# Windowed attention and a two-layer MoE product on one core: the globals of the second pair by one-hot products, three V casts moved ahead, and a split last store

## The chip, the cores and the metric

One core of a Trainium2 chip. The metric is the device time of one execution in microseconds (us), median of several runs. The engines are TensorE (PE, matrix products into PSUM), VectorE (DVE), ScalarE (ACT), GpSimd (POOL) and SyncE (SP, which here only issues transfers). Each works through its own instructions in order and waits on semaphores for the others. Transfers are issued from the queues of SP, ACT and GpSimd.

## The reference

```python
# q, k, v: (8, 8, 576, 64) float32; global_idx: 8 positions
scores = (1 / sqrt(64)) * q @ k.T                    # per batch and head
mask   = (|i - j| <= 32) | is_global[i] | is_global[j]
attn   = softmax(where(mask, scores, -1e9))
x      = (attn @ v) as (4608, 512)                   # heads side by side
r      = max(x @ w_in, 0)                            # w_in: (512, 2048)
out    = (s * r * r + b) @ w_out                     # w_out: (2048, 512)
```

## The kernel before

**Attention.** Two heads make a pair; a batch has 4 pairs, and there are 32 pairs in 8 batches. A pair's 576 positions go in 5 chunks of 120 keys, and each chunk's 128 partitions are 8 global keys and 120 own keys. `qk(p, s)` is the score product of chunk s (K columns as weights, Q of both heads as the moving operand), followed by `exp` on ACT into `e`; the product with the 0/1 mask on DVE into `em` is put off to the next step. `pv(p, parts)` sums over the chunks: part 0 with V (`vring`) as weights, the value product, and part 1 with ones, the sums, both into the one PSUM tile `po`. `norm_steps` turns the sums to reciprocals by two ACT steps (`ln`, `rep`), and DVE writes the normalised columns into `xt`. The 8 global queries of a batch are handled apart and put into `xt` by GpSimd in `scatter`, 8 small copies, once the batch's fourth pair is normalised.

**K and Q** of pairs 0 to 7 are loaded in bf16 as `six` and turned by PE: `trans_a` (K) and `trans_b` (Q), each 12 transposes into PSUM `pst`, then copies into `kt` (DVE, L444) and `qbd` (L460, one half by ACT and one by DVE). Q is kept block-diagonally in three buffers `qbufs`. Pairs 8 and on come by another way (`natk`, `natq`, rounded on ACT at L182).

**The globals' columns** of K and Q have to stand in every pair's `kt` and `qbd`. For pair 0 they are made by `select_first`: products of `six` with a one-hot matrix `sel6` (L678), copied from PSUM by DVE (L684, L689). For all later pairs `gather` fetches the global rows of all heads in a half of the batches by indirect DMA (`gf`), DVE rounds them (`gb`, L368, L387), PE turns them (L375), ACT copies them out as `gkt` and `gqd` (L379, L382), and `put_kq(p)` copies a pair's share into place (DVE, L415, L419). The global rows of V go through 16 small PE products (L394) into `gvx` (ACT, L396).

**V** of a pair is loaded as float32 into `natv` (ring of 4), cast into `vring` (ring of 4) by `cast_v` on ACT or GpSimd (L216), and then `put_v` writes the 8 global rows over it: by DVE, or (engine `None`) by a small SP transfer (L408).

**Order.** All is written out by hand; no scheduler moves anything. A list `later` holds what is to be issued one step later, and `now` what is issued at the end of the same step. Pair 0 to 4 run their five score steps in `first_pair`, without MoE work between; from there `run_pair` runs 8 steps (5 with scores, 3 with turning and casts), and `Q(n)` sets pieces of MoE work between them. `first_pair` also issues `warm`, products of a dummy tile of 512 columns whose results nobody reads. In order, the stretch in question is: turning of pair 0, one-hot products, masks; `first_pair(0)` with the rounding and turning of the gathered globals; the V globals; then GpSimd's transfers, and for pairs 1 to 3 a GpSimd cast followed by an SP transfer of the global V rows. GpSimd's queue between them holds the transfers of `win_t` (`moe_w_in`, two of 1 MB), `natv`, `six`, `wout_t`, and eight reads of the global positions into registers (L810). Software transfers of GpSimd wait for the one eight places before them.

**MoE.** Tokens go in tiles of 512: 16 products `psh` (L566) with ReLU on ACT (L573) and squaring on DVE (L576), then 4 output rows of 128 tokens `pso` (L581), each 16 products of 512 columns, scaled and biased on DVE into `osb` (L601) and stored by SP (L605).

Of the kernel before, what the change touches and what calls it, by code (L numbers as in the profile page):

```python
# [12 lines left out]
OP = mybir.AluOpType  # L13
# [53 lines left out]
def kernel(  # L67
# [385 lines left out]
    def trans_b(p, later=later):  # L453
        ps = trans("q", p)

        def evac():
            n = HB // NJ
            for hh, eng in ((1, nc.scalar.copy), (0, nc.vector.tensor_copy)):
                r = slice(D * hh, D * hh + D)
                eng(  # L460
                    out=view(qbufs[p % 3][r, hh], [P, NCH], [HB + NG, 2], [NJ, n], [1, NJ]),
                    in_=view(ps[r], [2 * n, NCH], [n, 2], [1, n], [NP6, NJ]),
                )

        later.append(evac)
# [85 lines left out]
    def moe_quanta():  # L551
        for t in range(NTOK // 512):
            c0 = 512 * t
            gl = []
            cols = []
            a = c0
            while a < c0 + 512:
                x0 = a % (NX * S)
                n = min(c0 + 512 - a, NX * S - x0)
                cols.append((x0, a - c0, n))  # L560
                a += n
            for f in range(16):
# [12 lines left out]
                gl.append(g)  # L575
                later.append(lambda g=g, r=r: nc.vector.tensor_mul(g[:], r[:], r[:]))  # L576
                yield
            for u in range(4):
                pso = ps_m.tile([P, DM], FP32, tag="moe", name="pso")
                for f in range(16):  # L580
                    nc.tensor.matmul(  # L581
                        pso[:], gl[f][:, u * P : u * P + P], wout_t[:, f],
                        start=(f == 0), stop=(f == 15),
                    )
                    if f % 4 == 3 and f < 15:
                        yield

                def store(pso=pso, r0=c0 + u * P, t=t):
                    if t < 3:
                        i = r0 // P  # L590
                        if i < 8:
                            osb = held.tile([P, DM], FP32, tag=f"held{i}", name="osbh")
                        else:

                            osb = six["kq"[i // 11]].rearrange("p n h j d -> p (n h j d)")
                            osb = osb.bitcast(FP32)[:, DM * ((i - 8) % 3) :][:, 0:DM]
                        held_rows.append((osb, r0))
                        nc.vector.tensor_scalar_mul(out=osb[:], in0=pso[:], scalar1=s_bc[:])
                        return
                    osb = mop.tile([P, DM], FP32, tag="osb", name="osb")  # L600
                    nc.vector.scalar_tensor_tensor(  # L601
                        out=osb[:], in0=pso[:], scalar=s_bc[:], in1=bias_row[:],
                        op0=OP.mult, op1=OP.add,
                    )
                    nc.sync.dma_start(out=out[r0 : r0 + P, :], in_=osb[:])  # L605

                later.append(store)
                yield

# [21 lines left out]
    def run_pair(p, nq, extra, turn):  # L631

        bi, hp = divmod(p, 4)
        if hp == 0 and p > 4:
            open_batch(bi)
        for s in range(8) if p > 4 else range(NCH, 8):
            prev, later[:] = list(later), []
            now = []
            if s < NCH:
                qk(p, s)  # L640
                if s in (1, 2):
                    step()
                if s == 4 and hp == 0 and bi > 1:
                    later.append(lambda: scatter(bi - 1))
                if s == 2 and p + 1 < NSIX:
                    cast_v(A, p + 1)
                if s == 2 and NSIX <= p + 2 < NPAIR:
                    cast_v(G, p + 2)
            elif s == 5:
                if p == 4:  # L650
                    cast_v(A, 5)
                if 4 < p < NSIX - 1:
                    trans_b(p + 1, now)
                elif turn:
                    turn_q(turn, now)
            elif s == 6 and 4 < p < NSIX - 1:
                trans_a(p + 1, now)
            for f in now + prev:
                f()
            if s == 0:  # L660
                pv(p - 1)
                pending.extend(norm_steps(p - 1))
            if s == 6 and p + 1 < NSIX:
                put_v(V, p + 1)
            for f in extra.get(s, ()):
                f()
            Q(nq[s])
# [1 line left out]
    def idle_bank():  # L669
        return ps_m.tile([P, DM], FP32, tag="moe", name="psw")  # L670

    def select_first():

        ps = ps_m.tile([P, 2, NG], FP32, tag="moe", name="psg")
        for i, t in enumerate("kq"):
            for j in range(NJ):
                for hh in range(2):
                    nc.tensor.matmul(  # L678
                        ps[D * hh : D * hh + D, i], six[t][:NP6, 0, hh, j], sel6[:NP6, j],
                        start=(j == 0), stop=(j == NJ - 1), skip_group_check=True,  # L680
                    )

        def put():
            nc.vector.tensor_copy(  # L684
                out=view(ktile[0], [P, NCH], [1, NG]), in_=view(ps[:, 0], [0, NCH], [1, NG])
            )
            for hh in range(2):
                r = slice(D * hh, D * hh + D)
                nc.vector.tensor_copy(  # L689
                    out=view(qbufs[0][r, hh, HB:], [P, NCH], [1, NG]),  # L690
                    in_=view(ps[r, 1], [0, NCH], [1, NG]),
                )

        later.append(put)
# [7 lines left out]
    def first_pair(p, extra={}):  # L702


        if p % 4 == 0:
            open_batch(p // 4)
        bank = idle_bank()
        for s in range(NCH):
            prev, later[:] = list(later), []
            now = []  # L710
            if p or s > 1:
                warm(1, bank)
            qk(p, s)
            if p == 4 and s > 2 or p < 4 and s < 2:
                (trans_b, trans_a)[1 - s % 2 if p == 4 else s](p + 1, now)
            if p and s in (1, 2 if p == 4 else 3):

                pv(p - 1, (int(s == 1),))
                if s == 1:
                    pending.extend(norm_steps(p - 1))  # L720
            if s == 3 and p < 4:
                step()
            for f in prev + now:
                f()
            for f in extra.get(s, ()):
                f()
            if s == 1:
                step()
                if p == 4:
                    step()  # L730
            if s == 4 and p == 4:
                put_v(V, 4)

    warm(8)
    trans_a(0)
# [22 lines left out]
            load_kq(4)  # L758
    clear(qbufs[1][0:D, 1], LQ)
    clear(qbufs[1][D:P, 0], LQ)  # L760
    select_first()
    flush()
    warm(3)
    vkey = const.tile([P, NCH], FP32)
# [21 lines left out]
    def clear_q2():  # L786
# [1 line left out]
        nc.vector.memset(qbufs[2][D:P, 0], 0.0)  # L788

    first_pair(0, {  # L790
        1: [lambda: cast_v(A, 0), lambda: build_masks((2,)), steps0[0]],
        2: [lambda: build_masks((3, 4))],
        3: [steps0[1], steps0[2]],
        4: [clear_q2, lambda: put_kq(1)],
    })
    for f in steps0[3:]:
        f()
    flush()
    put_v(V, 0)
    load_v(nc.gpsimd, 4)  # L800
    load_kq(5)
    cast_v(G, 1)
    put_v(None, 1)
    for p in (1, 2, 3, 4):
        first_pair(p)
        if p == 1:
            load_v(nc.gpsimd, 5)
            load_w_out(0)
            greg_p = [
                nc.gpsimd.value_load(g32[:1, i, 0:1], min_val=0, max_val=S - 1)  # L810
                for i in range(NG)
            ]
            cast_v(G, 2)
            put_v(None, 2)
        elif p == 2:
            load_kq(6)
            load_v(nc.gpsimd, 6)
            cast_v(G, 3)
            put_v(None, 3)
        elif p == 3:  # L820
            load_w_out(1)
            cast_v(G, 4)
    flush()
    scatter(0)
    for i in (1, 2, 3):
# [136 lines left out]
```

## Time and profile before

| | us |
|---|---|
| Median of 11 runs | 372.35 (371.67 to 373.1) |
| The profiled execution | 370.75 |
| its span | 369.1 |
| PE busy | 340.7 (92%) |
| DVE, ACT, POOL busy | 237.5, 227.3, 84.3 |

The span runs from the first instruction to the last event of the profile. Times in the views are counted from its start. A slice is a fortieth of the span, and a digit is the busy share in tenths. "Idle before" in brackets is the time for which the engine stood before an instruction, with what ended it. PEclk is the share of its full clock that PE was granted.

### The profile page before, as it was taken

The page shows a single profiled execution, that of the slowest core. Times are in us where ns is not written, and L with a number is a line of the kernel's source. Part 1 is how long each engine was busy: PE and PEld are TensorE (multiplying, and loading weights), DVE is VectorE, ACT ScalarE, POOL GpSimd, SP SyncE. Part 2 cuts the span into 40 slices and gives each one's busy share as a digit, 9 for nine tenths or more (in the row PEclk, how much of TensorE's full clock was granted, in tenths as well). Part 3 has the DMA queues.
Part 4 walks back from the last instruction along what each step waited for, and adds up shares of the span by engine and source line. Part 5 has one row for each costly group of instructions (what it writes and reads, how often), then busy time and mean ns, then how long its engine had stood idle before and what let it go on. Part 6 is the DMA issues. An engine that isn't in the chain of part 4 may idle for free.

```text
span 369.1 us, 7662 instructions
## 1 busy us (share of the span) xinstructions
PE 340.7 (92%) x2704; PEld 180.9 (49%) x2740; DVE 237.5 (64%) x634; ACT 227.3 (62%) x438; POOL 84.3 (23%) x165
## 2 busy tenths in 40 slices
PE   5774679899999999999999999999999999999995
PEld 2342334355545554557755555555557644444442
DVE  6774447666777789778777787777676743523521
ACT  6584538866776678667766776677648742612600
POOL 6965185103121311241303000401030001000000
PEclk9588789999999999999999999999999999999999
DMA  5999869999988897768568995995352011002002
GB/s 122 188 196 220 162 95 202 195 185 172 226 165 183 182 180 171 182 152 151 105 150 226 166 181 151 221 180 118 101 130 60 2 57 59 0 32 83 1 35 80
DMA packets 125991, 50.44 MB, mean 137 GB/s; under 512 B 113352, under 2 KB 118792, under 8 KB 125952
## 3 DMA queue, kind: packets, MB, share of 16 engines
q1 hardware_dynamic: 117056, 37.62, 49.8%
q0 software_dynamic: 8544, 12.03, 16.0%
q8 instruction: 21, 0.34, 0.4%
q10 hardware_dynamic: 352, 0.30, 0.3%
q14 instruction: 18, 0.15, 0.1%
HBM read 42.26 MB, written 9.44 MB: 140 GB/s over the span
## 4 chain that ended last, share of the span: by engine, by line
PE 77%; DMA 7%; issue 5%; POOL 4%; DVE 3%; ACT 2%; POOLq 1%; SPq 0%; ACTq 0%; DVEq 0%
PE pso L581 33%; PE psh L566 29%; PE po L495 7%; PE pss L469 5%; DMA natq<-in_q_dram 3%; DMA win_t<-in_moe_w_in_dram 3%; PE pst L196 2%; DMA natk<-in_k_dram 1%; POOLq L810 1%; POOL gf L291 1%; ACT r L573 1%; POOL xt L543 1%; POOL vring L216 1%; DVE g L576 1%; POOL sixq L155 1%
## 5 line engine op out<-in xcount | busy, mean ns | idle before, releaser
L566 PE MATMUL psh<-xt,win_t 128*128 128x512 bf16 (+4 forms) x691 | 139.3, 342 | 3.9 <-POOL xt L543 3.0
L581 PE MATMUL pso<-wout_t,g 128*128 128x512 bf16 x558 | 135.1, 379 | 1.6 <-issue 0.9
L573 ACT ACTIVATE r<-psh 128x512 bf16<-128x512 f32 x144 | 88.3, 614 | 59.6 <-PE psh L566 56.4
L473 ACT ACTIVATE e<-pss 128x384 bf16<-128x384 f32 (+1 forms) x160 | 76.9, 484 | 56.5 <-PE pss L469 56.1
L566 PEld LDWEIGHTS <-win_t 128*128 128x128 bf16 x704 | 64.1, 98 | 58.3 <-issue 5.8
L576 DVE TENSOR_TENSOR g<-r 128x512 bf16<-128x512 bf16 x144 | 59.3, 424 | 44.5 <-ACT r L573 44.3
L581 PEld LDWEIGHTS <-g 128*128 128x128 bf16 x576 | 54.8, 98 | 60.3
L476 DVE TENSOR_TENSOR em<-e,mask 128x384 bf16<-128x384 bf16 (+1 forms) x160 | 60.4, 380 | 30.5 <-ACT e L473 30.5
L469 PE MATMUL pss<-qbd,kt 128*128 128x384 bf16 (+1 forms) x160 | 52.3, 327 | 3.0 <-DVE qbd L419 2.1
L543 POOL COPY xt<-xg 128x4 bf16 x64 | 16.0, 250 | 102.3 <-DVE xt L532 98.9
L216 POOL CAST vring<-natv 128x640 bf16<-128x640 f32 x28 | 24.4, 873 | 61.4 <-PE po L495 42.6
L601 DVE SCALAR_TENSOR_TENSOR osb<-pso,s_bc,bias_row 128x512 f32<-128x512 f32 x24 | 18.0, 748 | 28.5 <-PE pso L581 28.4
L495 PE MATMUL po<-em,vring 128*64 128x160 bf16 (+3 forms) x448 | 20.0, 226 | 8.7 <-DMA vring<-gvx 8.3
L532 DVE TENSOR_TENSOR xt<-po,rep 128x600 bf16<-128x600 f32 x32 | 24.9, 779 | 1.4 <-ACT rep L529 0.9
L526 ACT ACTIVATE ln<-po 128x640 f32<-128x640 f32 x32 | 22.5, 703 | 5.0 <-PE po L495 4.8
L469 PEld LDWEIGHTS <-kt 128*128 128x128 bf16 x160 | 16.0, 100 | 19.2 <-DVE qbd L419 3.6
L495 PEld LDWEIGHTS <-vring 128*64 128x64 bf16 x448 | 15.7, 111 | 18.6 <-issue 9.7
L529 ACT ACTIVATE rep<-ln 128x640 f32<-128x640 f32 x32 | 24.1, 754 | 0.1
L204 DVE COPY qbd<-pst 64x600 bf16<-64x600 bf16 x48 | 22.2, 463 | 0.3
L495 PE MATMUL po<-em,onesb 128*64 128x160 bf16 (+2 forms) x448 | 19.1, 222 | 0.0
L182 ACT CAST natbq<-natq 120x640 bf16<-120x640 f32 x24 | 18.1, 752 | 0.0
L182 ACT CAST natbk<-natk 120x640 bf16<-120x640 f32 x24 | 17.7, 738 | 0.0
(107 smaller groups left out, 212.9 us busy)
## 6 DMA issues: line engine op xcount, KB each, us to landing
natv<-in_v_dram SPq DMA_DIRECT2D x55, 150.0 KB, 4.3
natk<-in_k_dram SPq DMA_DIRECT2D x47, 150.0 KB, 3.1
natq<-in_q_dram SPq DMA_DIRECT2D x47, 150.0 KB, 3.9
out_dram<-osb SPq DMA_DIRECT2D x24, 256.0 KB, 2.0
wst<-in_moe_w_out_dram POOLq DMA_DIRECT2D x8, 512.0 KB, 6.0
win_t<-in_moe_w_in_dram POOLq DMA_DIRECT2D x2, 1024.0 KB, 14.1
wout_t<-in_moe_w_out_dram POOLq DMA_DIRECT2D x4, 512.0 KB, 9.8
out_dram<-osbh SPq DMA_DIRECT2D x8, 256.0 KB, 4.0
```

Source lines behind the costliest of these rows:

```text
L182: nc.scalar.copy(out=natb[t][0:KC, p % NV].rearrange("p (c h d) -> p c h d", c=NCH, h=2), in_=nat[t][0:KC, p % NV],)
L216: eng(out=vring[:, p % NV], in_=natv[:, p % NV])
L469: nc.tensor.matmul(ps[:], ktile[p][:, P * c : P * c + P], qbufs[p % 3][:, :, LO[c] : HI[c]])
L473: nc.scalar.activation(e[:], ps[:], AF.Exp, scale=SCALE)
L476: later.append(lambda: nc.vector.tensor_mul(em[:], e[:], masks[c]))
L495: nc.tensor.matmul(po[D * hh : D * hh + D, a : a + n], onesb[:] if part else vring[:, p % NV, c, hh], emt[(p, c)][:, hh, x : x + n], start ...
L529: nc.scalar.activation(rep[:], ln[:], AF.Exp, scale=-1.0)
L532: lambda: nc.vector.tensor_tensor(out=view(xt[:, hp, x0:], [KC, NCH], [HB, 2], [1, HB]), in0=halves(po[:, 0:LQ]), in1=halves(rep[:]), op=O ...
L566: nc.tensor.matmul(psh[:, d0 : d0 + n], win_t[:, a, f * P : f * P + P], xt[:, a, x0 : x0 + n], start=(a == 0 and j == 0), stop=(a == 3), s ...
L573: nc.scalar.activation(r[:], psh[:], AF.Relu)
L576: later.append(lambda g=g, r=r: nc.vector.tensor_mul(g[:], r[:], r[:]))
L581: nc.tensor.matmul(pso[:], gl[f][:, u * P : u * P + P], wout_t[:, f], start=(f == 0), stop=(f == 15),)
```

## The change

1. `select_first()` becomes `select(p)` and is called for pairs 0 and 1, the second time in the last step of pair 0. Pair 1 no longer takes its columns from the gathered globals. These are rounded, turned and copied during pair 1 instead of pair 0, and pair 0's V globals are put in during pair 1.
2. Pair 1 is turned in steps 2 and 3 of pair 0 instead of 0 and 1, and pair 1 has one warm-up product instead of five.
3. GpSimd casts V of pairs 1, 2 and 3 in one go, before its next transfers; the three SP transfers of global V rows follow after pair 1. V of pair 4 is cast by ACT, and its global rows are put in one pair later.
4. For pairs 6 and 7 both halves of Q are copied by DVE; their V casts on ACT move from step 2 to step 5, and the global rows from step 6 to step 7.
5. The last output rows are made in two halves of 256 columns, with a store each, the second issued by ACT.

```diff
@@ trans_b
-            for hh, eng in ((1, nc.scalar.copy), (0, nc.vector.tensor_copy)):
+            for hh, eng in ((1, nc.scalar.copy if p < 6 else V), (0, V)):
@@ moe_quanta
-            for u in range(4):
+            parts = [(u, 0, DM) for u in range(4)]
+            if t == NTOK // 512 - 1:
+                parts[3:] = [(3, 0, DM // 2), (3, DM // 2, DM // 2)]
+            for u, n0, nn in parts:
                 pso = ps_m.tile([P, DM], FP32, tag="moe", name="pso")
                 for f in range(16):
                     nc.tensor.matmul(
-                        pso[:], gl[f][:, u * P : u * P + P], wout_t[:, f],
+                        pso[:, 0:nn], gl[f][:, u * P : u * P + P], wout_t[:, f, n0 : n0 + nn],
...
-                    nc.sync.dma_start(out=out[r0 : r0 + P, :], in_=osb[:])
+                    (nc.scalar if n0 else nc.sync).dma_start(
+                        out=out[r0 : r0 + P, n0 : n0 + nn], in_=osb[:, 0:nn]
+                    )
@@ run_pair
-                if s == 2 and p + 1 < NSIX:
-                    cast_v(A, p + 1)
...
             elif s == 5:
-                if p == 4:
-                    cast_v(A, 5)
+                if p + 1 < NSIX:
+                    cast_v(A, p + 1)
...
-            if s == 6 and p + 1 < NSIX:
+            if s == 7 and p + 1 < NSIX:
                 put_v(V, p + 1)
+            if s == 5 and p == 4:
+                put_v(V, p)
@@ select_first, now select(p)
-                        ps[D * hh : D * hh + D, i], six[t][:NP6, 0, hh, j], sel6[:NP6, j],
+                        ps[D * hh : D * hh + D, i], six[t][:NP6, p, hh, j], sel6[:NP6, j],
...
-                out=view(ktile[0], [P, NCH], [1, NG]), in_=view(ps[:, 0], [0, NCH], [1, NG])
+                out=view(ktile[p], [P, NCH], [1, NG]), in_=view(ps[:, 0], [0, NCH], [1, NG])
...
-                    out=view(qbufs[0][r, hh, HB:], [P, NCH], [1, NG]),
+                    out=view(qbufs[p][r, hh, HB:], [P, NCH], [1, NG]),
@@ first_pair
-            if p or s > 1:
+            if s > 1 if p == 0 else p > 1 or s == 0:
                 warm(1, bank)
             qk(p, s)
-            if p == 4 and s > 2 or p < 4 and s < 2:
-                (trans_b, trans_a)[1 - s % 2 if p == 4 else s](p + 1, now)
+            i = s - {0: 2, 4: 3}.get(p, 0)
+            if i in (0, 1):
+                (trans_b, trans_a)[i](p + 1, now)
...
             if s == 4 and p == 4:
-                put_v(V, 4)
+                cast_v(A, 4)
@@ the stretch after the masks of chunks 0 and 1
-        1: [lambda: cast_v(A, 0), lambda: build_masks((2,)), steps0[0]],
+        1: [lambda: cast_v(A, 0), lambda: build_masks((2,))],
         2: [lambda: build_masks((3, 4))],
-        3: [steps0[1], steps0[2]],
-        4: [clear_q2, lambda: put_kq(1)],
+        4: [clear_q2, lambda: select(1)],
     })
-    for f in steps0[3:]:
-        f()
     flush()
-    put_v(V, 0)
     load_v(nc.gpsimd, 4)
     load_kq(5)
-    cast_v(G, 1)
-    put_v(None, 1)
+    for p in (1, 2, 3):
+        cast_v(G, p)
     for p in (1, 2, 3, 4):
-        first_pair(p)
+        first_pair(p, {
+            0: [steps0[0], steps0[1]],
+            1: steps0[2:],
+            2: [lambda: put_v(V, 0)],
+        } if p == 1 else {})
         if p == 1:
+            for j in (1, 2, 3):
+                put_v(None, j)
             load_v(nc.gpsimd, 5)
             load_w_out(0)
...
-            cast_v(G, 2)
-            put_v(None, 2)
         elif p == 2:
             load_kq(6)
             load_v(nc.gpsimd, 6)
-            cast_v(G, 3)
-            put_v(None, 3)
         elif p == 3:
             load_w_out(1)
-            cast_v(G, 4)
```

More of the change, by code (lines that the diff above doesn't have):

```diff
@@ L581, in moe_quanta, with store @@
                     nc.tensor.matmul(
-                        pso[:], gl[f][:, u * P : u * P + P], wout_t[:, f],
+                        pso[:, 0:nn], gl[f][:, u * P : u * P + P], wout_t[:, f, n0 : n0 + nn],
                         start=(f == 0), stop=(f == 15),
                     )
-                    if f % 4 == 3 and f < 15:
+                    if (f + 1) % (4 * DM // nn) == 0 and f < 15:
                         yield
-                def store(pso=pso, r0=c0 + u * P, t=t):
+                def store(pso=pso, r0=c0 + u * P, t=t, n0=n0, nn=nn):
                     if t < 3:
@@ L601, in store @@
                     nc.vector.scalar_tensor_tensor(
-                        out=osb[:], in0=pso[:], scalar=s_bc[:], in1=bias_row[:],
-                        op0=OP.mult, op1=OP.add,
-                    )
-                    nc.sync.dma_start(out=out[r0 : r0 + P, :], in_=osb[:])
+                        out=osb[:, 0:nn], in0=pso[:, 0:nn], scalar=s_bc[:],
+                        in1=bias_row[:, n0 : n0 + nn], op0=OP.mult, op1=OP.add,
+                    )
+                    (nc.scalar if n0 else nc.sync).dma_start(
+                        out=out[r0 : r0 + P, n0 : n0 + nn], in_=osb[:, 0:nn]
+                    )
                 later.append(store)
@@ L670, in idle_bank, with select @@
         return ps_m.tile([P, DM], FP32, tag="moe", name="psw")
-    def select_first():
+    def select(p):
         ps = ps_m.tile([P, 2, NG], FP32, tag="moe", name="psg")
@@ L760 @@
     clear(qbufs[1][D:P, 0], LQ)
-    select_first()
+    select(0)
     flush()
```

## The prediction

> **What bounds the kernel now.** I read the page's slices first, then the waits before 48 us, then the timeline around the longest wait, then windows with the granted clock.
>
> ```profile
> PE   5774679899999999999999999999999999999995
> ...
> PEclk9588789999999999999999999999999999999999
> DMA  5999869999988897768568995995352011002002
> ```
>
> A slice is 9.2 us. After six slices at 4 to 7 tenths TensorE (PE) is full, at 8 or 9, so only work taken from PE, or its last few microseconds, can shorten that part. In the six, DMA is at 9 in slices two to four. The waits of the first 48 us, PE alone:
>
> ```profile
> PE po L495 <- DMA vring<-gvx: 8.3, 2, 6.5
> PE psg L375 <- DVE gb L368: 1.7, 1, 1.7
> ```
>
> Two waits of the value product cost 8.3 us, one of them 6.5. The timeline shows how they arise:
>
> ```profile
> 21.08 0.83 POOL L216 CAST vring<-natv 128x640 bf16<-128x640 f32 x1
> ...
> 25.27 1.84 POOL L171 DMA_DIRECT2D natv<-in_v_dram  x2 [3.36 <-DMA win_t<-in_moe_w_in_dram]
> ...
> 28.08 0.61 PE L495 MATMUL po<-em,vring 128*64 128x160 bf16 x14 [1.86 <-DMA vring<-gvx]
> ...
> 31.88 0.84 POOL L216 CAST vring<-natv 128x640 bf16<-128x640 f32 x1 [3.98 <-DMA win_t<-in_moe_w_in_dram]
> ...
> 38.51 1.01 PE L495 MATMUL po<-em,vring 128*64 128x160 bf16 x14 [6.48 <-DMA vring<-gvx]
> ```
>
> GpSimd casts V of pair 1 at 21.08, then stands behind the window weights (win_t, until 25.27), issues transfers, reads the eight global positions (27.9 to 31.9, which the page puts down to win_t), and only then casts pair 2. SyncE issues the global rows of V after each cast, at 21.94 and 32.75, and PE gets them 6.1 and 5.7 us later. PE's clock is half before 21 us, then full:
>
> ```profile
> 8.00:20.00 12.00, 9.20 (x89) 4.40 (x89) 8.08 (x31) 6.99 (x16) 10.50 (x14) 0.50 1.18 190
> 22.00:26.00 4.00, 3.84 (x63) 2.21 (x62) 3.21 (x10) 3.94 (x9) 0.73 (x1) 1.00 1.18 199
> ```
>
> (The last three columns are clock, DMA share and GB/s.) It falls to 0.50 again from 36 to 41, in and after the long wait, and from 48.5 to 50, after the 3.0 us in which GpSimd scatters the first batch and PE is idle. So the first batch is bound by a chain of V casts, small transfers and issues, and every microsecond that it ends earlier should move the full slices forward.
>
> **Part 1: pairs 0 to 4.** Removed: pair 0's wait for the gathered globals. Pair 1's 24 one-hot products cost PE 0.82 (those of pair 0: 7.71 to 8.53) and DVE 0.52 (8.56 to 9.08). Moved: the gathered globals, their turning and the V globals go into pair 1; the casts of pairs 2 and 3 go next to that of pair 1, ahead of the GpSimd wait. There they take two times 0.8, 21.9 to 23.5, hidden since the next issue waits for win_t until 25.27 anyway; without that cover they would cost 1.6. I walk the changed order with the durations of before, at half clock until it would return.
>
> Pair 0: PE no longer stops at 13.8, ends its fifth score product near 14.0 and the one-hot products near 14.7. But DVE is late: its half of pair 1's Q waits for ACT's half (1.3 us in one such wait now), and ACT has two exps to 11.15, the V cast of 0.72 to 11.87, an exp of 0.49 to 12.36 and its half of 0.65 to 13.01. So DVE copies 13.05 to 13.83; then two masks 0.71, three em of 0.35, K 0.77, clearing 0.80 and the globals 0.52 end at 17.65. Pair 1 starts at 17.7 instead of 18.26: only 0.6 of the gain is left.
>
> Pair 1, with new waits: its first score ends at 18.2, exp at 18.64, pair 2's Q transposes (0.69) at 18.66, ACT's half of them at 19.37, DVE's at 20.18, and only then DVE casts the globals (0.23), to 20.4. The four turning products wait for that, and behind them on PE stand score 2 (to 21.25), K of pair 2 (0.69, to 21.75) and the sums (0.83, to 22.4). That is 1.8 us of idle PE where now a warm-up matmul runs. DVE copies that K to 22.57, its globals (0.35) to 22.92, and casts the V globals (0.19) to 23.1; their 16 products run at 23.15 to 24.15 (1.01), two scores after them to 24.85. ACT has the first one's exp (to 25.04) and then two copies of the V rows (1.05), to 26.1; DVE puts them into pair 0's V (0.47) at 26.6. The value product of pair 0 starts at 26.6, against 22.27: a loss of 4.3. SyncE's three issues wait for the same 26.1; behind them stand only the scalars and the padding of natb, 320 KB that start 9 us earlier and delay the loads beside them by 1.4 us at 222 GB/s, hidden as Q and K of pair 5 land at 34.65 and are needed near 41.
>
> Pairs 2 to 4: pair 2's first score product is at 28.2; from there to its value product is 2.8 us at full clock (23.39 to 26.2 now) and 4.7 at half, so PE is there between 31.0 and 32.9. Rows issued at 26.1 land at 32.2, with the 6.1 of now. I take 32.6. Pair 3's rows come 0.8 later each and are no wait. From that product to the last transpose of pair 4 is 17.4 us now (28.08 to 45.47), less the 6.48 of waiting and about 0.9 of half clock after it: 10.0. End 42.6 instead of 45.47: **2.8 us gained**. Bounds: at full clock and with rows landing in 2.0 us, as the output rows do (nearest row for an undisturbed one), PE is there at 31.0 and the gain is 4.4; with 6.7 (the slowest small transfer here, b_bc), an issue at 27 and half clock (10.9), the end is 44.6 and the gain 0.9.
>
> Pair 1's four missing warm-up matmuls save PE nothing that shows, since it waits there. The granted clock was 0.50 until 21 and back at full only about 3 us after dense work began at 38.5. The Trainium skill ("TensorE: Matmul & The Clock Gate", What's actually happening) says that the clock is halved until a window of some 3.4 us was busy, which speaks against dropping them. By that rule alone pair 2 would run wholly at half clock and part 1 would bring 2.5 instead of 2.8, by estimate.
>
> Scatter, 3.0 us, and the MoE products follow as now, since SyncE's natk loads start behind a DVE step that moves along, and wout's second piece (44.30) is issued earlier too. Cast and row copy of pair 4's V go from GpSimd to ACT (0.72) and DVE (0.47): ACT stands idle 3.88 us before 50.41 and DVE 2.32 before 51.04. If that cover went, they would cost 1.2.
>
> **Part 2: pairs 5 to 7.** PE waits here:
>
> ```profile
> 58.43 0.45 PE L432 MATMUL pst<-ident,sixq 96*64 96x96 bf16 x12 [0.24 <-ACT e L473]
> ...
> 62.65 0.31 PE L469 MATMUL pss<-qbd,kt 128*128 128x320 bf16 x1 [0.59 <-DVE qbd L419]
> ...
> 68.98 0.45 PE L432 MATMUL pst<-ident,sixq 96*64 96x96 bf16 x12 [0.58 <-ACT e L473]
> ...
> 73.83 0.31 PE L469 MATMUL pss<-qbd,kt 128*128 128x320 bf16 x1 [1.13 <-DVE qbd L419]
> ```
>
> The V casts (0.74) leave the place where exp waits behind them, and the two ACT copies (0.65) become DVE copies (0.78) without the wait for ACT (1.07 each time now). For pair 6 DVE starts them near 58.75 and ends at 60.3 instead of 61.17; less the new order behind them, 0.45 is left at 62.65. For pair 7 the same brings about as much again. Sum **0.9**, between 0 (DVE, with 1.56 in one piece ahead of two g steps, becomes what PE waits for) and 2.5 (all four waits gone).
>
> **Part 3: the end.** The last product's 16 matmuls of 512 columns become 32 of 256. Splits exist in the trace: eight psh matmuls of a wrapped tile take 0.87, four whole ones 0.86, so four such groups add 0.04. DVE's last step of 512 columns takes 0.75 (365.01 to 365.76); half of it 0.42, gain 0.33. The last transfer, 2.0 us to landing with 256 KB, carries half, at best half the time after its issue of 0.33, gain 0 to 0.8; I take 0.2. ACT issues it; its queue is empty by then, and ACT and SyncE took 0.42 and 0.40 for the same issue at 0.86. Sum **0.5**, from 0.3 to 1.1.
>
> **Sum.** 2.8 + 0.9 + 0.5 = 4.2. The profiled execution took 370.75 (span 369.1 and 1.65 around it), so 366.5; it lies 1.6 under the median of 372.35, hence 368.2 for the median. Bounds of these terms: gain 1.2 to 8.0, of which the top needs every best case at once.
>
> **Rivals.**
>
> *The rows land late* (slower, 0.13). All three V transfers now start after 26.1, in the fullest DMA stretch. For: the V loads from GpSimd's queue at 17.91 took 14.2 us there. Against: four small SyncE transfers took 5.7 to 6.7. At 14.2 pair 2's product is at 40.3, the end of pair 4 at 50.3 to 51.2, 4.8 to 5.7 late; with parts 2 and 3 (1.4) that is 375.8 to 376.7. At 9.2 us part 1 is nothing (pair 4 ends at 45.3, as now), and from 10.6 the whole is slower. By the Trainium skill ("DMA: Bandwidth & Descriptors", Queues, rings and completion order) each DMA engine takes its queues in turn, packet by packet, so that SyncE's rows needn't stand behind all of GpSimd's loads; the rows of 6 us agree.
>
> *Pair 1 eats it all* (0.12). Pair 1 carries two new DVE and ACT chains, and my walk has already given 4.3 there; 2.8 more (half clock throughout, a missed buffer) and only parts 2 and 3 are left: 371.0.
>
> *Given back to the loads* (0.09). The 48 to 80 us stretch has DMA shares of 0.9 to 1.3, and the chain that ended last holds a natq transfer of 10.33 us from 52.46. If its end stays put, MoE starts early and waits there: gain of part 1 gone, and part 2 too, 371.9, no change. Against: these loads start by the same steps and DMA is idle (share 0.00) from 45.5 to 48.5.
>
> **How the numbers follow.** My forecast has 0.66, its own range 365.0 to 371.0. A fifth of the second rival falls within 0.2% (0.75 us, about what a measurement of this kernel can tell from no change), most of the third too. Faster: 0.66 + 0.10 + 0.02 = 0.78; same: 0.08; slower: 0.13 and 0.01 of the third. The range reaches over the rivals without loss to 372.2; left out are the slower one and the last of the best cases.
>
> **What would show it.** Right: V casts in a row near 21 to 24; no 6.48 wait at po; pair 0's value product near 26.6 and pair 4 done near 42.6, scatter at once; the waits at 62.65 and 73.83 (then 3 us earlier) halved; last DVE step near 0.42. Wrong: a po wait on vring over 3 us, a scatter later than 45.5, DVE qbd waits longer than now, or PE idle for natq, natk between 50 and 75.

## The result, and the profile after

The changed kernel takes 367.05 us (median of 8 runs, 364.93 to 371.18) where the kernel before takes 372.27 (31 runs on the same chip, 371.14 to 373.6): ratio 0.986, 95% interval 0.9839 to 0.9881. It is faster by 1.4%, as forecast; 368.2 was predicted. The profiled execution took 368.14, its span is 366.5. The comparisons here and below leave out executions that lie over 1.5% above the fastest of their kernel.

The slices of the page, those of before having been shown in the prediction:

```profile
PE   6759699899799999999999999999999999999996
PEclk9557989999999999999999999999999999999999
DMA  5999999999999787975559998894243011002002
```

TensorE (PE) has 9 for 4 in slice four and 9 for 7 in slice six, but 5 for 7 in slice three, and a 7 at slice eleven (91.6 to 100.8), where before there was a 9. The clock is half in slices two and three, one slice more than before, and DMA stands at 9 without a break up to slice thirteen.

Before, MoE started at 48.51, the products of `po` that summed pairs 1 and 2 having waited until 28.08 and 38.51:

```profile
48.51 0.58 PE L566 MATMUL psh<-xt,win_t 128*128 128x512 bf16 x1 [3.04 <-POOL xt L543]
```

The timeline of the changed kernel (start, duration, engine, line, operation, tiles; in brackets the idle time before and what ended it):

```profile
16.96 0.45 PE L469 MATMUL pss<-qbd,kt 128*128 128x320 bf16 x1 [2.07 <-DVE qbd L695]
20.05 0.31 PE L375 MATMUL psg<-ident,gb 64*64 64x64 bf16 x4 [1.69 <-DVE gb L368]
21.03 2.15 POOL L216 CAST vring<-natv 128x640 bf16<-128x640 f32 x3
23.46 1.01 PE L394 MATMUL psv<-gb,ident 128*8 128x64 bf16 x16 [1.23 <-DVE gb L387]
25.97 2.42 SPq L408 DMA_DIRECT2D vring<-gvx  x3
26.45 1.01 PE L495 MATMUL po<-em,vring 128*64 128x160 bf16 x14 [1.22 <-DVE vring L408]
32.72 0.61 PE L495 MATMUL po<-em,vring 128*64 128x160 bf16 x14
42.69 2.57 POOL L543 COPY xt<-xg 128x4 bf16 x8 [4.66 <-DVE xt L532]
45.31 4.44 PE L566 MATMUL psh<-xt,win_t 128*128 128x512 bf16 x11 [2.63 <-POOL xt L543]
```

The three casts stand in a row, the rows of V follow at 25.97, pair 0's value product starts at 26.45, and the next one (run in pair 2, summing pair 1; the prediction calls it pair 2's) at 32.72 with no wait before it. MoE starts at 45.31 instead of 48.51. Later:

```profile
60.86 0.25 PE L375 MATMUL psg<-ident,gb 64*64 64x64 bf16 x4 [0.62 <-DVE gb L368]
69.66 0.31 PE L469 MATMUL pss<-qbd,kt 128*128 128x320 bf16 x1 [0.96 <-DVE qbd L419]
98.06 0.30 PE L469 MATMUL pss<-qbd,kt 128*128 128x320 bf16 x1 [1.93 <-DVE qbd L419]
```

The second line is that of 73.83, 4.17 earlier. The first and the third are new. DVE stands behind a transfer there: at 60.86 behind the gathered globals (`gf`), at 98.06 behind `kt`, K of a later pair, turned by a transfer from SyncE's queue.

I cut the span at marks that every profile has: MoE's start, the score product of 69.66 (M1), the next that waits so (107.73 here, 109.81 before, M2), PE's end, the span's end. All in us; "after, again" is a second profile of the changed kernel. The rows are one execution each; casts_p23 and onehot_only ran on a second chip, casts_p23_kq5 and warms_fill on a third.

| kernel | MoE starts | to M1 | M1 to M2 | M2 to PE's end | to the span's end | span |
|---|---|---|---|---|---|---|
| before | 48.51 | 25.32 | 35.98 | 255.17 | 4.12 | 369.1 |
| after | 45.31 | 24.35 | 38.07 | 255.20 | 3.57 | 366.5 |
| after, again | 45.48 | 23.71 | 35.98 | 255.19 | 3.54 | 363.9 |
| no_part2 | 45.73 | 26.46 | 35.98 | 255.20 | 3.53 | 366.9 |
| casts_only | 43.34 | 25.86 | 35.98 | 255.16 | 4.16 | 364.5 |
| casts_p23 | 42.62 | 24.98 | 35.98 | 255.71 | 3.51 | 362.8 |
| casts_p23_kq5 | 42.96 | 24.99 | 35.99 | 255.19 | 3.57 | 362.7 |
| onehot_only | 49.61 | 25.70 | 35.99 | 255.57 | 3.53 | 370.4 |
| warms_fill | 45.29 | 24.25 | 38.56 | 255.19 | 3.51 | 366.8 |

So the profile's gain of 2.6 is 3.2 up to MoE, 1.0 up to M1, 0.55 at the end, and 2.1 given back between M1 and M2.

### The profile page after: what moved, and what is told of

It reads as the page before. It is cut to its first block, busy times and chain, and to the rows that moved or that the text cites. A ratio compares the mean times of both kernels' runs of the same rounds, so it can differ in the third digit from the quotient of the medians.

```text
span 366.5 us, 7742 instructions
## 1 busy us (share of the span) xinstructions
PE 342.8 (94%) x2741; PEld 182.9 (50%) x2776; DVE 240.2 (66%) x638; ACT 226.4 (62%) x437; POOL 83.2 (23%) x164
## 4 chain that ended last, share of the span: by engine, by line
PE 75%; DMA 9%; POOL 4%; issue 4%; DVE 3%; ACT 2%; POOLq 1%; SPq 0%; ACTq 0%
PE pso L585 34%; PE psh L566 27%; PE po L495 7%; PE pss L469 5%; DMA win_t<-in_moe_w_in_dram 3%; DMA wout_t<-in_moe_w_out_dram 3%; DMA kt<-natbk 2%; PE pst L196 2%; DMA natk<-in_k_dram 1%; POOL natv L171 1%; POOLq L819 1%; POOL gf L291 1%; POOL sixk L155 1%; POOL sixq L155 1%; DVE qbd L460 1%
## 5 line engine op out<-in xcount | busy, mean ns | idle before, releaser
L585 PE MATMUL pso<-wout_t,g 128*128 128x512 bf16 (+1 forms) x574 | 135.2, 373 | 1.6 <-issue 1.0
L585 PEld LDWEIGHTS <-g 128*128 128x128 bf16 x592 | 56.4, 98 | 59.0
L605 DVE SCALAR_TENSOR_TENSOR osb<-pso,s_bc,bias_row 128x512 f32<-128x512 f32 (+1 forms) x25 | 18.2, 727 | 28.0 <-PE pso L585 27.9
L182 ACT CAST natbk<-natk 120x640 bf16<-120x640 f32 x24 | 17.7, 738 | 0.0
```

The lines of the kernel that those rows point to most:

```text
L182: nc.scalar.copy(out=natb[t][0:KC, p % NV].rearrange("p (c h d) -> p c h d", c=NCH, h=2), in_=nat[t][0:KC, p % NV],)
L585: nc.tensor.matmul(pso[:, 0:nn], gl[f][:, u * P : u * P + P], wout_t[:, f, n0 : n0 + nn], start=(f == 0), stop=(f == 15),)
```

## The experiments

Two theories. *The chain*: the attention of the first batch is bound by casts, small transfers and copies; what they lose, the time loses. *The loads*: from 50 us on the transfers set the pace, and an earlier start of MoE is given back there.

### The change again, and its parts taken out (one chip)

**after_again**: the changed kernel once more.

> The changed kernel once more, as the measure for the others. Theory one (chain): the first batch's chain of casts and rows was the bound before 48 us and PE is the bound after it, so what the chain wins stays won; ratio near 0.986. Theory two (loads): the transfers between 48 and 110 us are a second limit close behind PE; part of the executions then give 1 to 3 us back in a wait for a K transfer, as the profiled one did at 98.06 (1.93 us), and the executions lie some 4 us apart.

367.99 us (365.65 to 375.89), ratio 0.9889 (0.9861 to 0.9918). Its profiled execution took 365.65 and has neither the wait of 0.62 nor that of 1.93: together 2.55, and the two profiled executions differ by 2.49. The five runs that are compared fall at 365.65 and 365.93, and at 367.67, 368.31 and 368.43. So the loads took back about 2.5 in one of the two profiled executions and nothing in the other, and the times suggest the same of the rest. The same transfer in both kernels' timelines, the changed one first:

```profile
88.62 3.99 SPq L189 DMA_TRANSPOSE kt<-natbk  x1
```

```profile
86.49 1.23 SPq L189 DMA_TRANSPOSE kt<-natbk  x1
```

SyncE came to it 2.1 later and its issue took 3.99 instead of 1.23. The chain of waits of the changed kernel says when it was done:

```profile
88.62 9.10 DMA kt<-natbk
97.74 0.18 DVE kt L415
```

9.10 from issue to landing, where the page's median of the 24 such transfers is 2.6. Two loads of 512 KB (`wst`, GpSimd's queue) ran beside it, issued at 86.54 and 87.94; but in the execution that did not wait the same two were issued at 86.07 and 87.48, beside the same transfer.

**casts_only**: the kernel before, with nothing but the casts moved.

```diff
-    cast_v(G, 1)
-    put_v(None, 1)
+    for p in (1, 2, 3):
+        cast_v(G, p)
+        put_v(None, p)
...
-            cast_v(G, 2)
-            put_v(None, 2)
...
-            cast_v(G, 3)
-            put_v(None, 3)
```

> The kernel before with nothing changed but the V casts of pairs 1, 2 and 3 and their row transfers next to each other ahead of the GpSimd transfers. Pair 1 starts at 18.3 and pair 0's value product at 22.3 as before; rows land near 28, 29 and 30, so that the 6.48 wait goes and pair 4 ends near 38.1 instead of 45.5. Theory one (chain): all of it is kept, 7.4 us, 364.9 (ratio 0.980), faster than the whole change; the one-hot products of pair 1 then cost more than they bring. Theory two (loads): the MoE starts near 41 but PE waits for loads between 50 and 110 us, over 4 us in sum, and the time is 367 to 370 (0.986 to 0.994).

365.07 us (363.86 to 366.12), ratio 0.9812 (0.979 to 0.9835). This small part beats the whole change, on the same chip, by 2.9 us, and the intervals do not meet. Its timeline:

```profile
21.52 2.30 POOL L216 CAST vring<-natv 128x640 bf16<-128x640 f32 x3
22.39 2.42 SPq L408 DMA_DIRECT2D vring<-gvx  x3
24.15 0.61 PE L495 MATMUL po<-em,vring 128*64 128x160 bf16 x14
28.14 0.61 PE L495 MATMUL po<-em,vring 128*64 128x160 bf16 x14
32.09 0.61 PE L495 MATMUL po<-em,vring 128*64 128x160 bf16 x14
38.70 0.45 PE L432 MATMUL pst<-ident,sixq 96*64 96x96 bf16 x12 [1.77 <-DMA sixq<-in_q_dram]
43.34 0.58 PE L566 MATMUL psh<-xt,win_t 128*128 128x512 bf16 x1 [3.35 <-POOL xt L543]
```

With the V globals made in pair 0, as before, the rows go at 22.39, 3.6 earlier than in the changed kernel, and no value product shows a wait for one (that of pair 1 landed at 28.00, just ahead of the product at 28.14). What is late next is the load of pair 5's Q, and then GpSimd, which is still issuing loads when it should scatter. So MoE came at 43.34 and not at the 41 that I had expected.

**no_part2**: the changed kernel with the old second batch (Q by ACT and DVE, V cast in step 2, global rows in step 6; the diff is cut).

```diff
-            for hh, eng in ((1, nc.scalar.copy if p < 6 else V), (0, V)):
+            for hh, eng in ((1, nc.scalar.copy), (0, V)):
...
+                if s == 2 and 4 < p < NSIX - 1:
+                    cast_v(A, p + 1)
...
```

> The changed kernel with the old second batch: Q of pairs 6 and 7 copied by ACT and DVE, their V casts in step 2. Theory one: the PE waits of 0.24, 0.59, 0.58 and 1.13 us near pairs 6 and 7 are back, and the time is 0.9 us over the changed kernel (ratio 0.988 to 0.989). Theory two: a later start of pairs 8 to 11 meets the loads with less wait, and the time is that of the changed kernel within 0.3 us.

367.05 us (366.24 to 368.59), ratio 0.9869 (0.9846 to 0.9892): by the time, the part brings nothing. By the profile it does: the four waits of before are back (0.29, 0.60, 0.59, and 1.13 in place of 0.89 in after_again), 1.7 more in sum. The table has 26.46 up to M1 without it and 23.71 with it, but the clock has a part in that: MoE's first 5 us ran at 0.50 here and at 0.66 there, 0.8 us by estimate (5 times the difference). Before and casts_only, with the same second batch, stand at 25.32 and 25.86. Its profile, without the later load waits, spans 366.9, and the changed kernel seems to lose 2.5 to them in three of its five. Inconclusive on the time.

**no_wst**: the changed kernel without the second load of `w_out`; its bias sums come from the bf16 copy that is there.

```diff
-        wt = stage.tile([P, 2, DM], FP32, tag="wst", name="wst")
-        nc.gpsimd.dma_start(out=wt[:], in_=w_out2[:, 2 * j : 2 * j + 2])
...
-            lambda i=i: nc.vector.tensor_add(out=wsum[:], in0=wsum[:], in1=wt[:, i])
+            lambda i=i: nc.vector.tensor_add(
+                out=wsum[:], in0=wsum[:], in1=wout_t[:, 2 * j + i]
+            )
...
```

> The changed kernel without the second load of w_out (8 transfers of 512 KB from 86 us on): the column sums for the bias are added up from the bf16 weights that lie in SBUF already, by as many DVE additions in the same steps. Theory one: transfers are not a bound, no change, ratio 0.986 within 0.001. Theory two: the wait of 1.93 at the fourth score product after 90 us goes, the K transfer lands in 3 to 4 us instead of 9.1, and the time is 1 to 2 us less, ratio 0.981 to 0.984, with executions closer together.

366.8 us (365.79 to 368.62), ratio 0.9875 (0.9846 to 0.9903). The waits near 98 and 107 are gone from its profile, but the rounded globals are waited for near 61, by 2.65 instead of 0.62. One load wait was exchanged for another, and the time is the same.

### The parts put together otherwise (a second chip, before 374.77 there)

**onehot_only**: the changed kernel, with the casts and rows of pairs 2 and 3 in their old places.

```diff
-    for p in (1, 2, 3):
-        cast_v(G, p)
+    cast_v(G, 1)
...
+            cast_v(G, 2)
+            put_v(None, 2)
...
+            cast_v(G, 3)
+            put_v(None, 3)
```

> The changed kernel with the V casts and rows of pairs 2 and 3 back in their old places; one-hot products for pair 1, the second batch and the split end stay. If the moved casts are what the first part gains by: pair 2's cast comes behind GpSimd's register reads again, near 32, its row lands near 38, and pair 2's value product waits to 38.5 as before; the first part then brings nothing (MoE near 48.5), and the second batch and the end leave 0.5 to 1.4, ratio 0.996 to 0.999. If the one-hot products gain something of their own (pair 1 starting 1.3 earlier), MoE starts near 47 and the ratio is about 0.993. Rows of pair 1 are issued after 26.1 and not at 22; should they be late, the ratio is above 1.

371.86 us (370.89 to 374.38), ratio 0.9932 (0.9908 to 0.9956). The long wait is there again:

```profile
34.33 0.72 POOL L216 CAST vring<-natv 128x640 bf16<-128x640 f32 x1 [4.00 <-DMA win_t<-in_moe_w_in_dram]
...
39.93 1.01 PE L495 MATMUL po<-em,vring 128*64 128x160 bf16 x14 [4.80 <-DMA vring<-gvx]
```

The cast of pair 2 is at 34.33, 2.45 later than in the profile of before, since GpSimd got past win_t at 27.71 instead of 25.27. Counted from that cast, MoE starts 15.28 later (16.63 before), so this kernel gains 1.35 there; 1.0 of it is a row that reached PE 5.60 after its cast instead of 6.63. The measured ratio says 2.5 (0.0068 of 374.77), about what was given for a gain by the one-hot products (0.993), but MoE's start was not the 47 given with it. The end brings 0.59 by the table. The second batch's edits bring nothing in this profile: 25.70 up to M1 against 25.32 before, with ACT standing for 2.50 ahead of 57.50 for no reason that the profile shows. So what makes up the 2.5 is not shown; the kernel before was not profiled on this chip, and whether win_t was as late there is not known. What is shown: without the moved casts PE waits 4.80 again, and pair 1's longer way hides behind that.

**casts_p23**: casts_only, with the second batch and the split end of the change, and V of pair 4 cast by ACT; globals and warm-up products as before. The diff is against casts_only, cut, since its other lines are those of the change:

```diff
-            for hh, eng in ((1, nc.scalar.copy), (0, nc.vector.tensor_copy)):
+            for hh, eng in ((1, nc.scalar.copy if p < 6 else V), (0, V)):
...
-            cast_v(G, 4)
```

> The moved casts and rows of pairs 1 to 3, the second batch's edits and the split end, without the one-hot products of pair 1. Theory one (what the chain loses, the time loses): the moved casts alone stood at 0.981 of the kernel before (MoE starts at 43.34); the second batch's edits bring up to 0.9 and the split end 0.5 on top, so about 363.7, 0.977, with MoE at 43.3, the waits on qbd near 58.0 and 69.2 smaller than 0.6 and 1.13, and 3.6 instead of 4.1 from PE's end to the span's end. Theory two (after 50 us the loads set the pace, however early MoE starts): only the split end counts, 0.980, and PE waits for loads (kt, gb or a value product's V) somewhere between 50 and 110 for as much as the second batch gained.

364.75 us (363.84 to 365.93), ratio 0.9752 (0.9721 to 0.9783): theory one, better than its 0.977. Against casts_only MoE to M1 is 0.9 shorter and the end 0.65, near the prediction's parts 2 and 3. For the 0.9 that is in part chance: MoE's first 5 us ran at a clock of 0.67 here and 0.56 there, and here ACT stood for 1.84 ahead of 49.79 for no reason that the profile shows. No load wait shows in this profile after 45.

**casts_p23_gather**: the same, with the second half's globals gathered at once after the scatter.

```diff
+    gather(1)
     load_w_out(2)
...
-        if p % 8 == 4 and p + 4 < NPAIR:
+        if p % 8 == 4 and 4 < p < NPAIR - 4:
```

> The same with the gathering of the second half's globals issued right behind the first batch's scatter, ahead of the loads that stand before it on GpSimd's queue. Theory one: no such wait of weight, so the same time as without it, within 0.2%. Theory two: PE's wait for the rounded globals near 61 (0.62 in one run of the changed kernel, 2.65 in one without the second load of w_out) comes from that queue; it is gone here, and the time is 0.6 to 2.6 lower where it stood, or the wait moves to a load that was issued behind it.

365.64 us, ratio 0.975 (0.971 to 0.979): no difference. casts_p23 had no wait for the globals to remove, so whether the queue caused it elsewhere stays open. Its profiled execution, at 370.09 the longest of the six, waits 1.20 at 85.66 and 3.19 at 98.15 behind the same kind of transfer as the 1.93 above: such a wait is not the changed kernel's alone.

**warms**: the changed kernel with pair 1's four dummy products.

```diff
-            if s > 1 if p == 0 else p > 1 or s == 0:
+            if p or s > 1:
```

> The changed kernel with the four dummy products of pair 1 put back (one ahead of each of its score products). It asks what the half clock up to 32 costs. If the missing dummy products keep the clock down and this costs time: full clock comes back near 21 to 24 as in the kernel before, pair 2's value product is there by 31 instead of 32.7, and the time falls by 1 to 1.7 (ratio 0.984 beside 0.989). If PE only waits there for V's rows and DVE's copies: the clock may rise, but pair 2's value product stays within 0.5 of 32.7, MoE starts within 0.5 of 45.4, and the time is the same within 0.3%.

369.03 us (366.22 to 371.26), ratio 0.9862 (0.9817 to 0.9908); the clock was 0.67 from 8 to 20 and 0.50 from 20 to 32 all the same, the product that sums pair 1 at 33.54 (32.72 in the changed kernel) and MoE at 46.14, both later than either case had it. Putting the dummy products back restored neither the clock nor the time.

### The clock, and the best version (a third chip, before 372.27 there)

**warms_fill**: dummy products in the gaps themselves.

```diff
-                warm(1, bank)
+                warm(4 if p == 1 else 1, bank)
...
+                if p == 1 and s == 0:
+                    warm(3, bank)
...
+                if p == 1 and s == 3:
+                    warm(2, bank)
...
+                    if p == 1:
+                        warm(2, bank)
```

> The changed kernel with dummy products put where TensorE stands idle in pair 1: four ahead of its first score product, three ahead of the turning of the globals, two ahead of the turned V globals and two ahead of pair 0's value product (idle there now: 2.07, 1.69, 1.23 and 1.22). It asks what the half clock from 15 to 32 costs. If the clock costs: it returns before 26, the stretch from pair 0's value product (26.45) to pair 2's (32.72), 6.27 at half clock, shrinks by 1.5 to 1.9, MoE starts near 43.6 and the ratio is about 0.983. If the rows of V bound that stretch (issued at 26.1, by the 5.7 to 6.1 of the kernel before), the clock returns but pair 2's value product stays near 32 and MoE near 45, ratio 0.986 to 0.989. If the dummy products get in the way of the real ones, later than that.

369.39 us (365.63 to 374.19), ratio 0.9904 (0.9873 to 0.9935). Windows and the one wait that matters (columns: window, length, busy time of PE, PEld, DVE, ACT, POOL with counts, clock, DMA share, GB/s):

```profile
20.00:29.00 9.00, 8.08 (x82) 4.33 (x82) 4.63 (x12) 4.67 (x12) 5.67 (x8) 0.52 1.14 198
29.00:33.00 4.00, 2.59 (x48) 1.44 (x43) 2.67 (x8) 3.47 (x7) 0.29 (x1) 1.00 1.19 234
```

```profile
32.70 0.61 PE L495 MATMUL po<-em,vring 128*64 128x160 bf16 x14 [1.41 <-ACT rep L529]
```

The clock came back at 29, three microseconds earlier than in the changed kernel, and nothing came of it: PE was ready 1.41 earlier, and waited. The view puts the wait down to `rep`, which ended at 32.62. But the product does not need it: in the changed kernel it ran at 32.72, ahead of the same `rep` (33.21). What it needs is the row of V of pair 1. By the trace's own records of landings (the views do not list them) that row, issued at 26.20, was there at 32.57, and the product 0.13 later, the same distance as in both waits of before (27.95 and 28.08, 38.38 and 38.51). Two other kernels with this front show the wait under its own name, the first of them no_part2, the other no_wst with 1.08:

```profile
33.14 0.61 PE L495 MATMUL po<-em,vring 128*64 128x160 bf16 x14 [0.91 <-DMA vring<-gvx]
```

So the row is the bound there, as the second of the three cases had it. In after_again, warms, no_part2, no_wst and here it landed at 32.57 to 33.41, and the product followed 0.13 or 0.14 later (in after_again and warms PE came just then and shows no wait). Only in the first profile of the changed kernel it was early, at 31.63; there PE's own products at half clock took until 32.72, which cost up to 1.0 by estimate (32.72 less 31.63 and 0.13). The product started at 32.70 for 32.72 and MoE at 45.29 for 45.31. From 20 to 29 the clock stayed at 0.52 here, so what the half clock costs ahead of the row's issue is not shown.

**casts_p23_kq5**: the loads of pair 5's K and Q ahead of pair 4's V.

```diff
-    load_v(nc.gpsimd, 4)
     load_kq(5)
+    load_v(nc.gpsimd, 4)
```

> The kernel with the moved casts, the second batch and the split end, without the one-hot products, and with the load of pair 5's K and Q issued ahead of pair 4's V instead of behind it. Its TensorE waited 2.38 at 38.67 for the Q of pair 5, which landed at 38.62, last of the three. If the order of the queue decides: Q of pair 5 lands near 36.9, the wait is under 0.7, MoE starts near 40.8 instead of 42.6, and the ratio falls from 0.975 to 0.970 or 0.971, less what the later loads take back. If the transfers share the engines whatever the order, the wait stays near 2 and the ratio at 0.975. V of pair 4 lands near 38.6 instead of 36.9; its cast stands behind the fifth score step near 40, so it should not be waited for.

362.93 us (362.08 to 364.38), ratio 0.9752 (0.9719 to 0.9784). The wait for Q fell from 2.38 to 1.05, between the two values expected, and what it saved was waited for elsewhere:

```profile
37.69 0.45 PE L432 MATMUL pst<-ident,sixq 96*64 96x96 bf16 x12 [1.05 <-DMA sixq<-in_q_dram]
42.96 1.01 PE L566 MATMUL psh<-xt,win_t 128*128 128x512 bf16 x2 [3.98 <-POOL xt L543]
```

PE waited 3.98 for the scatter instead of 2.08. GpSimd started it at 40.86, after issuing two V loads (38.24) and a piece of `wout_t` (40.08), while pair 3's columns in `xt` were done by 37.80. Here the scatter is bound by GpSimd's queue.

**casts_p23_gather_nowst**: casts_p23_gather without the extra loads of `w_out`; the edit is that of no_wst.

> The kernel with the early gathering, and without the eight extra loads of w_out for the bias sums (they are summed from the copy that is there already, rounded to bf16). In runs of the kernels before it the time scattered by 2 to 7 us, with a wait of 1.9 or 3.2 near 98 for K of a later pair, whose turning transfer stood beside two of these 512 KB loads. If those loads are the cause: no wait over 0.5 between 70 and 130, the spread under 2 us and the ratio about 0.970 (1.6 to 2 us below 0.975). If something else gives the time back: a wait of like size for another load, a spread as wide, ratio 0.975.

363.12 us (360.81 to 364.02), ratio 0.9748 (0.9713 to 0.9784). No wait over 0.21 after M1 in its profile, yet the spread is 3.2 and the ratio is that of casts_p23. The extra loads are not shown to be the cause.

**all_parts**: both of the last two.

> Both of the last two together. If each removes its own wait, the gains add: MoE near 40.8, no load wait after, ratio 0.965 to 0.967. If MoE's earlier start runs into the loads of pairs 6 to 9, what the order of pair 5's load brings is lost between 50 and 110 and the ratio is that of the kernel without the extra loads, about 0.970.

362.16 us (361.15 to 362.63), ratio 0.9723 (0.9693 to 0.9754): the fastest median, 1.4% below the changed kernel by the ratios, though its interval overlaps those of the kernels just before it. The gains did not add to 0.965: PE never waits for Q, and the scatter bounds again:

```profile
37.34 1.82 POOL L171 DMA_DIRECT2D natv<-in_v_dram  x2 [0.56 <-DMA sixq<-in_q_dram]
37.42 0.77 DVE L532 TENSOR_TENSOR xt<-po,rep 128x600 bf16<-128x600 f32 x1
39.16 0.80 POOL L345 DMA_DIRECT2D wout_t<-in_moe_w_out_dram  x1
39.93 2.21 POOL L543 COPY xt<-xg 128x4 bf16 x8
42.19 1.44 PE L566 MATMUL psh<-xt,win_t 128*128 128x512 bf16 x3 [3.95 <-POOL xt L543]
```

The columns are ready at 38.19; GpSimd is issuing until 39.9. Moving these issues behind the scatter was not tried.

## Why the prediction was right, point by point

**Part 1** was put at 2.8 and measured 3.2 at MoE's start. The walk held: pair 1's start 17.7 (16.96 measured), the turning 20.4 (20.05), the V globals 23.15 (23.46), pair 0's value product 26.6 (26.45), the rows 26.1 (25.97), the product in pair 2 32.6 (32.72), the last transposes' end 42.6 (42.68). The other 0.4 is the scatter, 2.63 of waiting instead of 3.04, which I had left as it was.

Behind 32.6 stood two limits, the row's landing at 32.2 and PE's own products between 31.0 and 32.9. Both are near the mark. In this profile the row landed at 31.63, 5.66 after its issue, and PE came to 32.72 through its own products at half clock; in the five other profiles with this front the row landed 6.37 to 7.00 after its issue, for the 6.1 that I had taken, and was the last to come. The bound of 4.4 (full clock, rows in 2.0) had no basis in its second half: none of these row transfers landed in less than 4.7.

**The clock rule.** The profile shows 0.50 from 20 to 32, with waits of 2.07, 1.69, 1.23 and 1.22 on PE up to 26.45. The Trainium skill ("TensorE: Matmul & The Clock Gate", What's actually happening) says that the clock is halved until a window of some 3.4 us was busy; this trace agrees, and the half clock went on through pair 2 as I took it to by that rule. Its price of 0.3 is neither shown nor ruled out: in warms_fill MoE started 0.02 earlier, but with a row that landed 0.94 later.

**Part 2** was put at 0.9; up to M1 the changed kernel is 0.97 shorter (with 0.62 lost to the globals' load), 1.61 in the other profile. The waits of 0.24, 0.59 and 0.58 went, 1.13 became 0.96 or 0.89, which makes 1.6 too. So the term was too small. It is not there in every execution: onehot_only, with ACT's stand of 2.50, has none of it.

**Part 3** was put at 0.5 and is 0.55. The step took 0.75 before, and the DVE half 0.48, not 0.42:

```profile
362.96 0.48 DVE L605 SCALAR_TENSOR_TENSOR osb<-pso,s_bc,bias_row 128x256 f32<-128x256 f32 x1 [1.26 <-PE pso L585]
```

**The rivals.** The rows did not land late by that rival's measure (7.00 at most, where 9.2 would have undone part 1). Pair 1 ate no more than the walk gave it. *Given back to the loads*, to which I gave 0.09, is partly true, and I had it in the wrong place: not a stop between 50 and 75, but 0.62 at 60.86 and 1.93 at 98, in some executions, about 2.5 in all. That term is missing from my sum. The profiled execution therefore took 368.14 where I had 366.5, and the second one, which escaped the loads, 365.65, which is 5.1 below the profile of before. The medians (372.27 and 367.05) differ by 5.2, more than the 4.2 of the sum. That the forecast lies only 1.2 off is in part luck: parts 1 and 2 brought 1.1 more than their terms, and the loads took up to 2.5 back. The kernel before was profiled once; whether such waits are in others of its runs (371.14 to 373.6) is not shown.

**What the prediction did not see** is where the gain sits. It counted pair 0's value product, 4.3 later, as a price inside part 1, but never asked what the casts would do without it. The casts alone gain 5.2 up to MoE (48.51 to 43.34); the one-hot globals with their moves, on top of casts moved already, cost 2.1 to 3.5 of it (45.5 to 46.0 against 43.34 on the first chip, 46.14 against 42.62 on the second, 45.29 against 42.96 on the third, the last two pairs with other small edits between them). The price is paid at the row of pair 1: on the first chip it is issued at 22.39 and lands at 28.00 in casts_only, in after_again at 25.96 and 32.75. With the casts in their old place this price is not seen, as onehot_only shows.

## What to carry to other kernels

When a change joins several edits, walk each alone as well as all together: two edits that both relieve one wait do not add, and the second can cost what the first has gained. An instruction that other queues wait for (here a cast of 0.8) belongs ahead of any issue that can block its queue. And when the front gets faster, ask what becomes the next bound: here first the load of Q, then the scatter behind issues on the same queue, and further back a transfer that is usually hidden.

## What the runs showed of the hardware

The clock is not a matter of the program alone. casts_p23 and casts_p23_kq5 differ by the order of loads that GpSimd issues from 17.86 on; from 8 to 17 they were granted 0.52 and 1.00. The product that sums pair 1 started at 27.55 and 27.90 all the same, in both 0.13 or 0.14 after its row had landed, and MoE at 42.62 and 42.96: where a transfer was the bound, half the clock was no loss.

Beside a full stream of loads a small transfer is slow. The rows of V issued by SyncE before MoE's start, 10 KB each, took 4.7 to 7.2 us from issue to landing (DMA share 1.1 to 1.2 from 22 to 34), the last store of SyncE, 128 KB at a share of 0.2, 1.7.

The turning transfer of K, 2.6 usually, took 9.10 in one execution, of which 3.99 was its issue on SyncE's queue; in another of the same program the issue took 1.23 and nobody waited. What decided it is open: it came after loads from the same queue and beside two large ones from GpSimd's, but so did the other, and kernels without the two large ones were no faster.
